# Attention and feed-forward in one kernel: the low part of q on GpSimd, and a later place for one pair's split

## The chip, the cores and the metric

The kernel runs on one core of a Trainium2 chip. The metric is the device time of one execution in microseconds. Five engines work side by side, each through its own queue in order: TensorE (PE in the profile; PEld is its weight load), VectorE (DVE), ScalarE (ACT), GpSimd (POOL) and SyncE (SP), which issues the DMAs. [...]

## The reference, cut to what matters

Causal attention over 4 batches, 12 heads, 448 positions and a head size of 64, and then, per position, a layer norm, two matrix products with a ReLU between them, and a residual:

```python
scores = scale * np.matmul(q, k.transpose(0, 1, 3, 2))
scores = np.where(mask, -1000000000.0, scores)
scores = scores - np.max(scores, axis=-1, keepdims=True)
attn = np.exp(scores)
attn = attn / (np.sum(attn, axis=-1, keepdims=True) + 1e-09)
x = np.matmul(attn, v)              # heads joined: 4 x 448 x 768
xn = (x - mu) / np.sqrt(var + 1e-06) * g_ln
out = x + np.maximum(xn @ w_ch1, 0.0) @ w_ch2    # 768 -> 3072 -> 768
```

## The kernel before, in words

**Slots.** The feed-forward part (`ffn`, L409) is cut into 48 slots per batch; a slot is 18 matmuls with 448 columns, and needs one half tile of weights. The main loop (L489) goes through slot numbers: negative ones are the head, in which batch 0's attention runs alone, and slots 0 to 191 carry the feed-forward of batches 0 to 3. At each slot it records, in this order, the steps in `pre`, the weights' steps, 18 feed-forward matmuls, and the steps in `post`. Each engine then does its own instructions in the order in which they were recorded; so the slot of a step sets its place in every queue, and no more than that: when it runs is settled by semaphores. The attention of batch b+1 is laid over the feed-forward of batch b.

**Exact products from fp32r matmuls.** Matmul operands are split in a high part (a copy that rounds to fp32r) and a low part (the difference). Weights: `wh` on ACT (L122), `wl` on DVE (L126), one slot ahead of use; while batch 0's feed-forward runs, the weights are also converted from 64-bit words (ACT L99 and L103, DVE L110). The hidden layer: `hh` on ACT (L426), `hl` on DVE (L427), which reads PSUM. The layer norm's output: `xh` on ACT (L358), `xl` on GpSimd (L361).

**Queries and keys of batches 1 to 3.** One pair of heads is loaded as `qkraw` (128 partitions, 4 x 448: two heads of q, two of k, each held twice, in partitions 0 to 63 and 64 to 127). `split1` (L186) makes `qs` as a rounded copy on ACT and `kh` as a rounded cast on DVE. `split2` (L196) subtracts: the lower 64 partitions of `qs` become the low part of q (L200, DVE), and `kl` becomes the low part of k (L203, GpSimd). A scores matmul with `kh` and one with `kl` (L234) then give the product. `qs`, `kh`, `kl` and `qkraw` have one buffer each. There are 18 such pairs. Batch 0 does without a split.

**Softmax.** `scores` (L205) writes negated, masked scores and their minimum on DVE (L242); `exps` on ACT (L256); `norm` (L262) makes the reciprocal of the sum on DVE (L267, L268) and scales four rows of blocks, on GpSimd for batch 0 and on DVE for the others (L272). Then come transposes on PE (L288) whose results ACT or DVE copies out (`PT`, L291 or L293), and the product with v (`px`, L303).

**Where steps stand.** In `steps` (L366) a pair p of batches 1 to 3 has `load` at 6p-4, `split1` at 6p-2 and `split2` at 6p-1, counted in a time of its own. `add_batch` (L456) maps that to slots. For batch 1 the negative times, which are those of its first pair alone, are moved by `FIRST` = -20: its load stands at slot -24, `split1` at -22 and `split2` at -21, in the middle of batch 0's attention. Its scores begin at slot -9. Batch 0's fifth pair has its normalisations at slots -22 and -20, the sixth and last at -16 and -14.

Of the kernel before, what the change touches and what calls it, by code (L numbers as in the profile page):

```python
# [32 lines left out]
EARLY = 45  # L33
GAP = 6
FIRST = -20
SAT0, TAT0, NAT0, END0, EV0 = [-1, 0, 2, 2, 4], [7, 8, 9, 10, 11], [4, 6], 13, [1, 1, 0, 1, 0]
SAT, TAT, NAT, END, EV = [0, 0, 1, 1, 2], [3, 4, 4, 5, 5], [3, 4], 6, [1, 1, 0, 0, 0]
EV1 = [1, 1, 1, 1, 1]
# [9 lines left out]
def kernel(ctx, tc, qk, v, w1, w2, g, out):  # L48
    nc = tc.nc
# [27 lines left out]
    def load_raw(s):  # L77
        kind, i = order[s // 2]
        raw[s] = sb.tile([P, UH, 2], U32, tag="raw", name="raw", bufs=5)
        src = (w1 if kind == "w1" else w2)[i].bitcast(U32)  # L80
        nc.sync.dma_start(
            out=raw[s].rearrange("p a b -> p (a b)"), in_=src[:, s % 2 * UE:(s % 2 + 1) * UE]
        )
# [40 lines left out]
    def split2(s):  # L124
        wl[s] = sb.tile([P, UH], F32R, tag="wl", name="wl", bufs=4)
        nc.vector.tensor_tensor(  # L126
            out=wl[s], in0=w32[s], in1=wh[s].bitcast(F32), op=ALU.subtract
        )

    def weights_ahead(start):  # L130


        early = 4
        todo = {}

        def put(t, *fs):
            todo.setdefault(max(t, start), []).extend(fs)

        for s in range(B * ns):
            t = (-EARLY + GAP * s, *ELAG) if s < early else (s - 4, 1, 2, 3)  # L140
            put(t[0] + t[3], (split2, s))
            if s < ns:
                put(t[0], (convert1, s))
                put(t[0] + t[1], (convert2, s))
                put(t[0] + t[1] + 1, (keep, s))
                if s + 5 < ns:
                    put(t[0] + t[1] + 1, (load_raw, s + 5))
            elif s % 2 == 0:
                put(s - 8, (load_full, s))
            put(t[0] + t[2], (split1, s))  # L150
        rank = [split2, convert2, convert1, keep, load_raw, load_full, split1]
        for fs in todo.values():
            fs.sort(key=lambda f: rank.index(f[0]))
        return todo


    class Att:
# [38 lines left out]
        def split2(self, p):  # L196
            r = self.t.pop(("raw", p))
            qs, kh, kl = self.t["qk", p]
            rq, rk = r[:, 0:2, :], r[:, 2:4, :]
            nc.vector.tensor_tensor(  # L200
                out=qs[D:], in0=rq[D:], in1=qs[D:].bitcast(F32), op=ALU.subtract
            )
            nc.gpsimd.tensor_tensor(out=kl, in0=rk, in1=kh.bitcast(F32), op=ALU.subtract)  # L203
# [246 lines left out]
    with tc.manual_schedule():  # L450
        more_qk = sb.tile([P, KC, S], F32, tag="xh", name="more_qk", bufs=1)
        first_qk = sb.tile([P, HF, S], F32, tag="hh", name="first_qk")
        rest = sb.tile([P, HF * S], F32, tag="hl", name="rest")
        pre, post, att = {}, {}, {}

        def add_batch(b):  # L456
            att[b] = Att(b)
            first, second, end = att[b].steps()
            shift = b * ns - end - (1 if b else 0)

            def slot(t):
                if b != 1:
                    return t + shift
                if t < 0:
                    return t + FIRST
                return t - 2 + HOLE[0] if t <= 2 else t - 3 + HOLE[1]

            for mine, whole in ((first, pre), (second, post)):
                for t, fs in mine.items():
                    whole.setdefault(slot(t), []).extend(fs)  # L470
            return slot(min(min(first), min(second)))

        start = add_batch(0)
        for p in range(NP):
            att[0].load(p)
            if p >= 2:
                load_raw(p - 2)
        nc.sync.dma_start(out=g_sb, in_=g)
        make_identity(nc, ident)
        nc.gpsimd.memset(mask, 0.0)  # L480
        nc.gpsimd.affine_select(
            out=mask[:, S - C:], in_=mask[:, S - C:], compare_op=ALU.is_ge, fill=-8.0e9,
            base=0, pattern=[[-1, C]], channel_multiplier=1,
        )
        nc.gpsimd.memset(mhalf, -0.5)
        for s in range(4, 5):
            pre.setdefault(start + 6 + 4 * s, []).append((load_raw, (s,)))
        feed, ahead = None, weights_ahead(start)
        for s in range(start, B * ns):  # L489
            for b in range(1, B):  # L490
                if b not in att and s >= (b - 1) * ns - (-start if b == 1 else 8):
                    assert add_batch(b) >= s, (b, s)
            for f, args in pre.get(s, []):
                f(*args)
            for f, x in ahead.get(s, []):
                f(x)
            if s >= 0:
                if s == 0:
                    hh = sb.tile([P, HF, S], F32R, tag="hh", name="hh")
                    hl = sb.tile([P, HF, S], F32R, tag="hl", name="hl")  # L500
                if s % ns == 0:
                    feed = ffn(att[s // ns], s, hh, hl)
                next(feed)
            for f, args in post.get(s, []):
                f(*args)
        for _ in feed:
            pass
# [33 lines left out]
```

## Time and profile before

| | |
|---|---|
| median of 3 runs | 919.53 us (918.36 to 921.22) |
| the profiled execution | 919.61 us, span 917.8 us |
| PE busy | 897.9 us (98%), 4864 matmuls |
| PEld busy | 790.2 us (86%) |
| DVE busy | 553.8 us (60%) |
| ACT busy | 452.8 us (49%) |
| POOL busy | 121.8 us (13%) |

Busy shares are means over stages that differ. The head, up to some 80 us, is batch 0's attention; the stretch to some 300 us is batch 0's feed-forward with the conversion of the weights and batch 1's attention; then three more feed-forwards follow, two of them with attention beside them. PE's matmuls are pipelined and their ends are modelled, so its busy time hides small waits; those show in the idle time ahead of a weight load.

### The profile page before, as it was taken

What the parts mean: (1) busy time and instruction counts of PE and PEld (TensorE: products, weight loads), DVE (VectorE), ACT (ScalarE), POOL (GpSimd) and SP (SyncE); (2) the same over time, 40 slices, a digit from 0 to 9 for tenths busy, and PEclk for the clock granted to TensorE, in tenths of its full rate; (3) what the DMA queues carried; (4) which work ended last, traced back from release to release, by engine and by line L of the source; (5) the groups of instructions that cost most, each with busy time, mean ns of one, the idle gap of its engine ahead of it and who ended that gap; (6) DMA issues with size and microseconds to landing.
All of it is one profiled execution on the core that took longest, in us unless ns stands there. A gap on an engine that the chain in (4) does not pass through costs nothing.

```text
span 917.8 us, 12820 instructions
## 1 busy us (share of the span) xinstructions
PE 897.9 (98%) x4864; PEld 790.2 (86%) x4864; DVE 553.8 (60%) x1208; ACT 452.8 (49%) x907; POOL 121.8 (13%) x115
## 2 busy tenths in 40 slices
PE   6988999999999999999999999999999999999998
PEld 4656889888899988988889998888988999999997
DVE  4877788777778566655664676556664634333431
ACT  5955888778865544444442355433542333222320
POOL 5543111101021111100102210011100200000000
PEclk9998999999999999999999999999999999999999
DMA  9920778787778643333313634343222343323210
GB/s 245 338 76 22 287 260 281 282 305 248 254 258 272 232 154 110 109 123 119 103 48 123 214 126 151 120 152 111 84 96 77 120 148 116 120 104 104 103 65 31
DMA packets 35246, 144.36 MB, mean 157 GB/s; under 512 B 4080, under 2 KB 8688, under 8 KB 35184
## 3 DMA queue, kind: packets, MB, share of 16 engines
q1 hardware_dynamic: 35184, 143.54, 45.2%
q8 instruction: 38, 0.62, 0.3%
q14 instruction: 24, 0.20, 0.1%
HBM read 119.15 MB, written 24.38 MB: 156 GB/s over the span
## 4 chain that ended last, share of the span: by engine, by line
PE 88%; ACT 5%; DVE 4%; DMA 1%; issue 1%; SPq 1%; POOL 0%; ACTq 0%
PE po L440 38%; PE ph L421 34%; PE px L303 5%; PE sc L234 4%; PE pt L288 4%; ACT P L256 2%; PE pln L316 1%; DMA raw<-w_dram 1%; PE sc L227 1%; ACT w L99 1%; ACT bits L103 1%; ACT wh L122 1%; DVE P L272 1%; DVE hl L427 1%; DVE wl L126 1%
## 5 line engine op out<-in xcount | busy, mean ns | idle before, releaser
L421 PE MATMUL ph<-xh,wh 128*128 128x448 f32 x576 | 214.5, 372 | 1.4 <-ACT xh L358 1.4
L440 PE MATMUL po<-hh,wh 128*128 128x448 f32 x576 | 214.1, 372 | 0.0
L421 PE MATMUL ph<-xl,wh 128*128 128x448 f32 x576 | 211.7, 368 | 0.5 <-POOL xl L361 0.5
L421 PE MATMUL ph<-xh,wl 128*128 128x448 f32 x576 | 211.3, 367 | 0.2
L440 PE MATMUL po<-hh,wl 128*128 128x448 f32 x576 | 210.7, 366 | 0.0
L440 PE MATMUL po<-hl,wh 128*128 128x448 f32 x576 | 210.6, 366 | 0.0
L427 DVE SCALAR_TENSOR_TENSOR hl<-ph,hh 128x448 fp32r<-128x448 f32 x96 | 59.8, 624 | 145.6 <-ACT hh L426 145.6
L122 ACT ACTIVATE wh<-full 128x768 fp32r<-128x768 f32 x144 | 119.3, 838 | 53.7 <-PE po L440 50.8
L126 DVE TENSOR_TENSOR wl<-full,wh 128x768 fp32r<-128x768 f32 x144 | 136.4, 953 | 0.8 <-ACT wh L122 0.5
L426 ACT ACTIVATE hh<-ph 128x448 fp32r<-128x448 f32 x96 | 52.0, 543 | 153.4 <-PE ph L421 153.2
L256 ACT ACTIVATE P<-P,nm 112x448 f32<-112x448 f32 (+3 forms) x176 | 91.7, 523 | 68.0 <-DVE nm L242 68.0
L421 PEld LDWEIGHTS ph<-xh,wl 128*128 128x128 f32 x576 | 108.6, 189 | 10.6 <-DVE wl L126 2.2
L421 PEld LDWEIGHTS ph<-xh,wh 128*128 128x128 f32 x576 | 108.7, 189 | 10.3 <-ACT xh L358 1.7
L421 PEld LDWEIGHTS ph<-xl,wh 128*128 128x128 f32 x576 | 108.7, 189 | 8.9 <-POOL xl L361 1.0
L440 PEld LDWEIGHTS po<-hh,wl 128*128 128x128 f32 x576 | 108.1, 188 | 9.2 <-DVE wl L126 0.4
L440 PEld LDWEIGHTS po<-hh,wh 128*128 128x128 f32 x576 | 108.2, 188 | 8.5
L440 PEld LDWEIGHTS po<-hl,wh 128*128 128x128 f32 x576 | 108.4, 188 | 8.2
L242 DVE CUSTOM_DVE_ANT_0 P<-sc,mask 112x448 f32<-112x448 f32 (+3 forms) x176 | 70.6, 444 | 51.9 <-PE sc L234 39.6
L203 POOL TENSOR_TENSOR kl<-qkraw,kh 128x896 fp32r<-128x896 f32 x18 | 51.8, 2878 | 377.0 <-DVE kh L193 370.3
L444 DVE TENSOR_TENSOR xT<-po,xT 128x448 f32<-128x448 f32 x48 | 29.9, 623 | 112.7 <-PE po L440 112.7
L288 PE MATMUL pt<-ident,P 112*112 112x112 f32 x440 | 55.1, 262 | 3.8 <-ACT PT L291 2.6
L288 PEld LDWEIGHTS pt<-ident,P 112*112 112x112 f32 x440 | 46.9, 134 | 13.5 <-ACT PT L291 4.1
(63 smaller groups left out, 941.8 us busy)
## 6 DMA issues: line engine op xcount, KB each, us to landing
full<-scratch SPq DMA_DIRECT2D x72, 768.0 KB, 4.2
raw<-w_dram SPq DMA_DIRECT2D x48, 768.0 KB, 5.7
scratch<-w SPq DMA_DIRECT2D x48, 384.0 KB, 2.9
qkraw<-qk_dram SPq DMA_DIRECT2D x18, 896.0 KB, 7.5
out_dram<-xT SPq DMA_DIRECT2D x24, 224.0 KB, 2.0
vt<-v_dram SPq DMA_DIRECT2D x18, 224.0 KB, 5.4
first_qk<-qk_dram SPq DMA_DIRECT2D x8, 224.0 KB, 5.5
rest<-v_dram SPq DMA_DIRECT2D x6, 224.0 KB, 7.8
```

Source lines behind the costliest of these rows:

```text
L122: nc.scalar.activation(out=wh[s], in_=w32[s], func=ACTF.Copy)
L126: nc.vector.tensor_tensor(out=wl[s], in0=w32[s], in1=wh[s].bitcast(F32), op=ALU.subtract)
L203: nc.gpsimd.tensor_tensor(out=kl, in0=rk, in1=kh.bitcast(F32), op=ALU.subtract)
L234: nc.tensor.matmul(pt[:, o:o + n], lhsT=qs[:, h, C * i:C * i + C], rhs=kk[:, h, :n], start=(part == 0), stop=(part == 1),)
L242: nc.vector.tensor_tensor_reduce(out=self.t["P", p, h][:, OFF[i]:OFF[i + 1]], in0=pt[:, o:o + n], in1=mask[:, S - n:], op0=ALU.add, op1=AL ...
L256: nc.scalar.activation(out=pp, in_=pp, func=ACTF.Exp, scale=-1.0, bias=nm[:, x:x + 1], accum_out=self.t["sm", p, h][:, i:i + 1],)
L288: nc.tensor.transpose(pt[:, o:o + C], pp[:, a:a + C], ident[:C, :C])
L303: nc.tensor.matmul(px[D * h:D * h + D, C * j:], lhsT=vt[:, h, j, :], rhs=self.t.pop(("PT", p, h, j)), start=(j == 0), stop=(j == NC - 1),)
L421: nc.tensor.matmul(pm[y], lhsT=w[:, c * P:c * P + P], rhs=z[:, c, :], start=(c == 0 and i == 0), stop=(c == KC - 1 and i == 2),)
L426: nc.scalar.activation(out=hh[:, x + y, :], in_=pm[y], func=ACTF.Relu)
L427: nc.vector.scalar_tensor_tensor(out=hl[:, x + y, :], in0=pm[y], scalar=0.0, in1=hh[:, x + y, :].bitcast(F32), op0=ALU.max, op1=ALU.subtract,)
L440: nc.tensor.matmul(pm, lhsT=w[:, o:o + P], rhs=z[:, x, :], start=(x == 0 and i == 0), stop=(x == HF - 1 and i == 2),)
```

## The change

`split2` issues both subtractions on GpSimd, that for q first, in all 18 pairs. For the first pair of batch 1 a table `PARTS` replaces the shift: `split1` stands at slot -18 instead of -22, and `split2` at -13 instead of -21. Its load stays at -24.

```diff
 FIRST = -20
+PARTS = [-18, -13]
...
             qs, kh, kl = self.t["qk", p]
             rq, rk = r[:, 0:2, :], r[:, 2:4, :]
-            nc.vector.tensor_tensor(
+            nc.gpsimd.tensor_tensor(
                 out=qs[D:], in0=rq[D:], in1=qs[D:].bitcast(F32), op=ALU.subtract
             )
             nc.gpsimd.tensor_tensor(out=kl, in0=rk, in1=kh.bitcast(F32), op=ALU.subtract)
...
                 if t < 0:
-                    return t + FIRST
+                    return PARTS[t + 2] if t >= -2 else t + FIRST
```

With the added line, the line numbers of the changed kernel are one higher. The names in the following pieces: `rest` and `P` hold the softmax rows, `sc` is a scores tile in PSUM, `nm` the minimum that L242 reads out after each piece of scores.

DVE in the head, after the reciprocals of the fifth pair's first head; before:

```order
L193 CAST kh<-qkraw 128x896
L242 ISA rest,nm<-sc,mask 112x112
L242 ISA nm 112x1
L242 ISA rest,nm<-sc,mask 112x336
L242 ISA nm 112x1
L200 TENSOR_TENSOR qs<-qkraw,qs 64x896
L293 COPY PT<-pt 112x448
L242 ISA P,nm<-sc,mask 112x448
```

and with the change:

```order
L243 ISA rest,nm<-sc,mask 112x112
L243 ISA nm 112x1
L243 ISA rest,nm<-sc,mask 112x336
L243 ISA nm 112x1
L294 COPY PT<-pt 112x448
L243 ISA P,nm<-sc,mask 112x448
```

The cast to `kh` and the subtraction are gone from in front of the `PT` copy; the cast stands further on, behind the scores of the next groups, and the subtraction is not on DVE any more. PE's queue and SP's queue have the same order as before, and on ACT the copy to `qs` moves back by nine instructions.

GpSimd in the head; before, from the first pair's `kl` on:

```order
L203 TENSOR_TENSOR kl<-qkraw,kh 128x896
L272 TENSOR_SCALAR rest<-rest,r 112x112
L272 TENSOR_SCALAR rest<-rest,r 112x224
L272 TENSOR_SCALAR rest<-rest,r 112x448
L272 TENSOR_SCALAR rest<-rest,r 112x336
L272 TENSOR_SCALAR P<-P,r 112x112
L272 TENSOR_SCALAR P<-P,r 112x224
L272 TENSOR_SCALAR P<-P,r 112x448
L272 TENSOR_SCALAR P<-P,r 112x336
```

and with the change, from the last head's normalisation on:

```order
L273 TENSOR_SCALAR P<-P,r 112x112
L273 TENSOR_SCALAR P<-P,r 112x224
L273 TENSOR_SCALAR P<-P,r 112x448
L273 TENSOR_SCALAR P<-P,r 112x336
L201 TENSOR_TENSOR qs<-qkraw,qs 64x896
L204 TENSOR_TENSOR kl<-qkraw,kh 128x896
L329 TENSOR_TENSOR ve<-ve,mhalf 112x4
L362 TENSOR_TENSOR xl<-xg,xh 128x448 x6
```

Both subtractions of the first pair stand behind the last normalisation of batch 0 and in front of the layer norm's `ve`.

DVE at the third pair of batch 1, from the cast on; before:

```order
L193 CAST kh<-qkraw 128x896
L126 TENSOR_TENSOR wl<-w_1177,wh 128x768
L110 SCALAR_TENSOR_TENSOR w_1282<-w_1282,bits 128x768
L427 SCALAR_TENSOR_TENSOR hl<-ph,hh 128x448
L200 TENSOR_TENSOR qs<-qkraw,qs 64x896
L126 TENSOR_TENSOR wl<-w_1231,wh 128x768
```

and with the change:

```order
L194 CAST kh<-qkraw 128x896
L127 TENSOR_TENSOR wl<-w_1177,wh 128x768
L111 SCALAR_TENSOR_TENSOR w_1282<-w_1282,bits 128x768
L428 SCALAR_TENSOR_TENSOR hl<-ph,hh 128x448
L127 TENSOR_TENSOR wl<-w_1231,wh 128x768
L111 SCALAR_TENSOR_TENSOR w_1333<-w_1333,bits 128x768
```

The `wl` that stood behind the subtraction follows `hl` directly. At the fourth and fifth pair there is no `hl` in this place: the cast is followed by a `wl`, a conversion, the subtraction (before only), a second `wl` and a second conversion. GpSimd has `qs` and then `kl` at each of these pairs.

## Rows read from the trace of the kernel before

**Rows 1.** the page: the span
```profile
span 917.8 us, 12820 instructions
```

**Rows 2.** who waited for whom, PE only: us in total, times, longest us
```profile
PE px L303 <- DVE PT L293: 2.4, 1, 2.4
```

**Rows 3.** the chain that ended last, 30 to 100 us: start us, us, what
```profile
46.22 0.85 ACT qs L192
47.09 0.15 DVE qs L200
47.24 3.90 issue
51.14 0.64 DVE PT L293
```

**Rows 4.** timeline of POOL, 40 to 96 us: start, us, engine, line, operation
```profile
45.98 2.14 POOL L272 TENSOR_SCALAR rest<-rest,r 112x112 f32<-112x112 f32 x4 [2.09 <-DVE r L268]
48.08 2.08 POOL L203 TENSOR_TENSOR kl<-qkraw,kh 128x896 fp32r<-128x896 f32 x1
58.96 3.82 POOL L272 TENSOR_SCALAR P<-P,r 112x112 f32<-112x112 f32 x8 [3.61 <-DVE r L268]
```

**Rows 5.** one stretch: us, busy us of PE, PEld, DVE, ACT, POOL, then PEclk
```profile
53.00:57.00 4.00, 4.00 (x16) 2.98 (x15) 1.90 (x9) 3.12 (x12) 2.35 (x4) 0.57 0.61 242
```

**Rows 6.** timelines of DVE (54 to 58 us) and PE (67 to 69)
```profile
56.05 0.39 DVE L242 CUSTOM_DVE_ANT_0 P<-sc,mask 112x224 f32<-112x224 f32 x1 [1.86 <-PE sc L227]
...
67.91 0.36 PE L234 MATMUL sc<-kl,qs 128*112 128x448 f32 x1
```

**Rows 7.** POOL instructions by shape: xcount, busy us, mean ns, idle before
```profile
L203 POOL TENSOR_TENSOR kl<-qkraw,kh 128x896 fp32r<-128x896 f32 x18 | 51.8, 2878 | 377.0 <-DVE kh L193 370.3 <-PE ph L421 6.8
L171 POOL MEMSET first_qk<- 64x448 f32 x4 | 1.9, 466 | 0.4 <-POOLq L530 0.3
L480 POOL MEMSET mask<- 112x448 f32 x1 | 0.5, 476 | 0.0
```

**Rows 8.** timeline of DVE, 120 to 130 us
```profile
125.27 0.62 DVE L427 SCALAR_TENSOR_TENSOR hl<-ph,hh 128x448 fp32r<-128x448 f32 x1
125.91 2.40 DVE L200 TENSOR_TENSOR qs<-qkraw,qs 64x896 fp32r<-64x896 f32 x1
128.32 0.96 DVE L126 TENSOR_TENSOR wl<-w,wh 128x768 fp32r<-128x768 f32 x1
```

**Rows 9.** timeline of POOL, 90 to 330 us
```profile
94.24 2.63 POOL L203 TENSOR_TENSOR kl<-qkraw,kh 128x896 fp32r<-128x896 f32 x1 [6.77 <-PE ph L421]
...
123.76 3.60 POOL L203 TENSOR_TENSOR kl<-qkraw,kh 128x896 fp32r<-128x896 f32 x1 [26.88 <-DVE kh L193]
...
151.32 3.59 POOL L203 TENSOR_TENSOR kl<-qkraw,kh 128x896 fp32r<-128x896 f32 x1 [23.96 <-DVE kh L193]
...
210.75 3.60 POOL L203 TENSOR_TENSOR kl<-qkraw,kh 128x896 fp32r<-128x896 f32 x1 [25.89 <-DVE kh L193]
...
300.30 2.79 POOL L203 TENSOR_TENSOR kl<-qkraw,kh 128x896 fp32r<-128x896 f32 x1 [11.68 <-DVE kh L193]
...
326.05 2.72 POOL L203 TENSOR_TENSOR kl<-qkraw,kh 128x896 fp32r<-128x896 f32 x1 [22.96 <-DVE kh L193]
```

**Rows 10.** timeline of PE's weight loads, at six pairs
```profile
99.32 0.19 PEld L421 LDWEIGHTS ph<-xh,wl 128*128 128x128 f32 x1
...
129.33 0.19 PEld L421 LDWEIGHTS ph<-xh,wl 128*128 128x128 f32 x1 [0.46 <-DVE wl L126]
...
157.55 0.19 PEld L440 LDWEIGHTS po<-hh,wl 128*128 128x128 f32 x1
...
216.32 0.19 PEld L421 LDWEIGHTS ph<-xh,wl 128*128 128x128 f32 x1 [0.45 <-DVE wl L126]
...
305.80 0.19 PEld L421 LDWEIGHTS ph<-xh,wl 128*128 128x128 f32 x1
...
331.95 0.19 PEld L421 LDWEIGHTS ph<-xh,wl 128*128 128x128 f32 x1
```

## Prediction

> **What bounds the kernel.** The profiled execution took 919.61 us, with a span of 917.8 us [rows 1]; the median of the three runs is 919.53 us, so the sum below is made against 919.61 and nothing has to be added for the difference. About 0.3% (2.8 us) is what a measurement of this kernel can tell from no change. I read the waits of PE first: beside the first load there is one wait of any size in the whole execution, 2.4 us before the `px` matmuls, ended by a `PT` copy on DVE [rows 2]. PE otherwise works nearly without a break (DVE's weight halves come late to a few weight loads, below), so a change on DVE, ACT or POOL is worth something where it removes that wait, and costs something where it makes a new one.
>
> The chain of waits names what stands in front of the 2.4 us [rows 3]: ACT's copy `qs` (0.85 us), then DVE's subtraction for the low part of `qs`, in which 3.90 us go by as "issue", then the `PT` copy that PE needs. That subtraction is 64x896 elements and lasts 0.95 us where nothing is in its way (below); here it lasts from 47.09 to 51.11. GpSimd's timeline says why [rows 4]: four normalisations run from 45.98 to 48.12, and `kl` follows without a gap, 48.08 to 50.16. DVE's operation ends 0.95 us after `kl`. So an operation with two SBUF inputs on DVE stands still while GpSimd works in SBUF, and it did not get in between two GpSimd operations that followed each other closely. [...]
>
> **The change, part by part.**
>
> *The first pair's parts, 18 slots ahead instead of 22, and 13 instead of 21.* ACT's `qs` copy, DVE's `kh` cast and the two subtractions leave the stretch at 46 to 51 us. DVE's `PT` copy then stands behind scores that are ready, and PE's 2.4 us go. With them goes the reason for the low clock: 4.0 us at 0.57 [rows 5] are 4.0 x 0.43 = 1.7 us of lost matmul time. Together 2.4 + 1.7 = **4.1 us**. Floor: the 2.4 us alone, if the clock falls for another reason. Ceiling: the 0.85, 0.15 and 3.90 us of the chain, 4.9 us. I take 4.1, since both parts of it have their rows. What comes back later is covered: ACT's 0.85 us leaves its queue before one `PT` copy and comes back before another, nine operations on, so that ACT's own chain is as long as it was at the end of the head; DVE's `kh` cast now stands in front of the scores of the last pair, where DVE waited 1.86 us for PE [rows 6]. GpSimd's `qs` and `kl` come after its last normalisations, which end at 58.96 + 3.82 = 62.78 [rows 4]; two subtractions of 2.08 us bring that to 66.94, and the first matmul that reads `kl` starts at 67.91 [rows 6]. Both move forward together, so 1.0 us is spare; if the cover were gone, each microsecond would be PE's. On SP nothing moves.
>
> *The other 17 pairs: one subtraction from DVE to GpSimd.* What it costs GpSimd: the 128x896 `kl` has a mean of 2.88 us, but that holds waits; with none it takes 2.08 us (at 48.08) [rows 4, 7]. The new one has the same 896 elements in 64 partitions. GpSimd's own rows say whether half the partitions halve the time: a memset of 64x448 takes 466 ns, one of 112x448 476 ns [rows 7]. So I take 2.08 us, the bound below being 1.04. GpSimd has the time; but it holds up DVE while it works, and this is where the cost lies.
>
> Take the pair at 123 us. `kl` is asked for at 123.76, and DVE goes on through two more two-input operations without GpSimd getting in; at 125.27 DVE begins `hl`, which reads PSUM, and 2.08 us later, at 127.36, `kl` ends. DVE's `qs` begins at 125.91, stands still until 127.36 and ends 0.95 us later; the next `wl` ends at 129.28 [rows 8, 9]. PE loads it at 129.33, 0.46 us late [rows 10]. After the change DVE has `wl` in place of `qs`, at 125.9, and GpSimd has `qs` and `kl` in its queue. ACT's copy is done while DVE is still in its normalisations, so `qs` is asked for in the middle of DVE's row and waits, as `kl` did, until `hl` at 125.27. Then GpSimd works 4.16 us without a gap, and `wl` waits for all of it. So PE gets `wl` at the end of `kl` before, plus 2.08 (the second subtraction), plus 0.96 (`wl`), plus 0.05 to the load. By pair, from [rows 9, 10]:
> - 94.24: 96.87 + 3.09 = 99.96 against 99.32, costs 0.64 us.
> - 123.76: 130.45 against 129.33, costs 1.12 us.
> - 210.75: 217.44 against 216.32, costs 1.12 us.
> - 300.30: 306.18 against 305.80, costs 0.38 us.
> - 326.05: 331.86 against 331.95, still in time by 0.09 us; this and the ten pairs after it are counted as nothing, and this is the tightest cover in the sum.
>
> The pair at 151.32 and the one like it at 181 us are let off: behind DVE's weight conversion stands not `hl` but the next `wl` and conversion, so DVE, going from one two-input operation to the next as at 123.76, makes the `wl` that PE wants next before GpSimd gets in, and what is then held up is the `wl` of the slot after. Were they not let off, the first would cost 154.91 + 3.09 - 157.55 = 0.45 us [rows 9, 10], the other about as much. Loss 0.64 + 1.12 + 1.12 + 0.38 = **3.3 us**, at most 4.3. Who else waits: the first scores of a pair need both low parts, which are two slots of PE work ahead of them; the load of the next pair's `qkraw` waits 2 us longer, three slots ahead of its use. Neither is near.
>
> Sum: 919.61 - 4.1 + 3.3 = **918.8 us**.
>
> [...] At 47.09 DVE waited through the end of a normalisation (48.12) and through `kl` behind it [rows 3, 4]: the turn stayed with GpSimd over the boundary of two instructions. [...] The row decides for the forecast.
>
> **Rivals.**
> 1. *DVE gets a turn between GpSimd's `qs` and `kl`.* Then the first of the two stands where `kl` alone stood, `wl` follows at its end without DVE's own `qs` ahead of it, and PE's load comes at 127.36 + 0.96 + 0.05 = 128.37 instead of 129.33: the loss is gone and the waits of 0.46 and 0.45 us [rows 10] with it. 919.61 - 4.1 - 0.9 = 914.6 us. For it: a DVE operation that arrives just then could win; against it: DVE's 4.02 us at 47.09.
> 2. *GpSimd's `qs` gets its turn inside DVE's row of normalisations*, since it is now asked for as soon as ACT is done and not after `kh`. It decides from the point where `kh` and the `wl` behind it start 2.08 us late. At the pairs of 123 and 210 us, where PE waits for `wl` already, that is 2.08 us in place of 1.12 each, 1.9 more; at the two let off up to 2.08 each, of which I take half, 2.1 more. 918.8 + 4.0 = 922.8 us, slower than before. Against it: at 123.76 GpSimd waited through two DVE operations [rows 8, 9].
> 3. *Sixty-four partitions take half the time.* With 1.04 us the costs above shrink to 0.08 us at two pairs: 919.61 - 4.1 + 0.2 = 915.7 us. Against it: the two memsets.
>
> That the change does not do what it says is excluded by the order: all 18 subtractions stand on GpSimd, and the first pair's behind the last normalisation.
>
> **How the numbers follow.** Forecast 0.55, with its own range 917.2 (gain at its ceiling) to 920.4 (a loss of 4.3 and a gain of 3.5); rival 1 0.25, rival 2 0.12, rival 3 0.08. Faster by over 0.3% is under 916.9: rivals 1 and 3, and 0.03 of the forecast's edge, 0.36. Slower by over 0.3% is over 922.4: a little over half of rival 2 and 0.03 for a stretch that I have not seen, 0.10. The rest, 0.54, lies within. The range takes in rivals 1 and 3 and stops short of rival 2: 914.0 to 921.0.
>
> **What would show it.** Right: no PE wait over 1 us before `px` at 49 us and a clock of 1.00 from 53 to 57; the head, up to the first `ph` matmul, some 4 us shorter; GpSimd's `qs` at 2.1 us of work and `kl` right behind it; a `wl` at the 123 and 210 us pairs of some 3.5 to 4.5 us instead of 0.96, with a late weight load behind it; the weight conversion stretch, up to 300 us, 3 us longer. Wrong: a `wl` that stands between `qs` and `kl` (rival 1), a `kh` or normalisation of 2.4 us or more on DVE (rival 2), a `qs` of 1 us on GpSimd (rival 3), or PE waiting for `kl` before the first scores.

## The result, and the profile after

The changed kernel took 927.86 us (median of 4 runs, 927.69 to 930.9) against 920.38 us for the kernel before in the same comparison: a ratio of 1.0094, with a 95% interval from 1.0073 to 1.0114 (the two medians alone give 0.8%). The forecast was 918.8 us and the range ended at 921.0; slower by over 0.3% had been given 0.10. The profiled execution took 927.78 us with a span of 926.0 us, 8.2 us more than before [rows 1].

The page of the profile after: the span, the busy line (busy us, share of the span, instructions) and GpSimd's share in 40 slices of the span, in tenths.

```profile
span 926.0 us, 12865 instructions
PE 898.7 (97%) x4864; PEld 787.1 (85%) x4864; DVE 561.7 (61%) x1190; ACT 453.0 (49%) x907; POOL 163.9 (18%) x133
POOL 5555023302022122210202320121200300000000
```

PE has the same work to do; GpSimd has 42 us more, in the stretches with attention. Waits of PE behind DVE have appeared (who waited for whom, PE only: us in total, times, longest):

```profile
PE ph L422 <- DVE wl L127: 4.5, 8, 0.6
PE pt L289 <- DVE P L273: 3.1, 5, 1.1
PE po L441 <- DVE wl L127: 1.7, 3, 0.6
```

The 2.4 us in front of `px` [rows 2] are gone; in their place PE waits eleven times for `wl` and five times for the normalised rows `P`.

**The head.** Clock and busy time of the stretch that was at 0.57 before [rows 5], now:

```profile
53.00:57.00 4.00, 4.00 (x30) 2.83 (x29) 1.96 (x10) 2.74 (x10) 2.87 (x7) 1.00 0.00 0
```

The `px` product with the old wait inside it, and its neighbours, on PE's timeline, before:

```profile
39.68 2.11 PE L303 MATMUL px<-PT,rest 112*64 112x448 f32 x16
...
47.87 1.53 PE L303 MATMUL px<-PT,rest 112*64 112x448 f32 x6
51.82 1.35 PE L303 MATMUL px<-PT,rest 112*64 112x336 f32 x10 [2.42 <-DVE PT L293]
...
59.12 2.37 PE L303 MATMUL px<-PT,rest 112*64 112x448 f32 x16
```

and after:

```profile
39.18 2.11 PE L304 MATMUL px<-PT,rest 112*64 112x448 f32 x16
...
47.36 2.11 PE L304 MATMUL px<-PT,rest 112*64 112x448 f32 x16
...
54.24 2.43 PE L304 MATMUL px<-PT,rest 112*64 112x448 f32 x16
```

From the start of the second to the start of the third it was 11.25 us (the second stands in two parts, with the wait between them) and is 6.88 us: 4.4 us won where 4.1 were forecast. The other gain lies around it. Some 0.5 us lie behind, where PE's granted clock over 70 to 92 us is 0.92 instead of 0.84. And 0.5 us are there already at the first of the three products (39.18 against 39.68), ahead of the first instruction that the change moves, so they are not its work: in the profiled executions of the kernels in this document that product starts anywhere from 37.55 to 39.68 us, with the same work in front of it. Why it varies is open; a difference of up to 2 us between two profiles in the head can be this.

**The rest.** To see where the time goes, take the weight load that is the first of a slot to read `wl`. The slots with loads at 305.80 and 331.95 stand in [rows 10]; the first and a late one before:

```profile
81.45 0.34 PEld L421 LDWEIGHTS ph<-xh,wl 128*128 128x128 f32 x1
...
665.13 0.19 PEld L421 LDWEIGHTS ph<-xh,wl 128*128 128x128 f32 x1
```

and the same four slots after:

```profile
75.97 0.19 PEld L422 LDWEIGHTS ph<-xh,wl 128*128 128x128 f32 x1
...
305.43 0.19 PEld L422 LDWEIGHTS ph<-xh,wl 128*128 128x128 f32 x1
...
332.74 0.19 PEld L422 LDWEIGHTS ph<-xh,wl 128*128 128x128 f32 x1
...
673.30 0.19 PEld L422 LDWEIGHTS ph<-xh,wl 128*128 128x128 f32 x1
```

So the changed kernel is 5.5 us ahead at slot 0, 0.4 us ahead when batch 1's pairs and the first of batch 2 are through (305.43 against 305.80), 0.8 us behind one pair later, and 8.2 us behind at the last pair of batch 3 (673.30 against 665.13), after which nothing changes. The pairs up to 305 us cost 5.1 us, where 3.3 were forecast; the eleven behind them cost 8.5 us, where nothing was.

One of these pairs on GpSimd after, the one at 326.05 before [rows 9]:

```profile
324.26 2.12 POOL L201 TENSOR_TENSOR qs<-qkraw,qs 64x896 fp32r<-64x896 f32 x1 [19.95 <-ACT qs L193]
327.62 2.71 POOL L204 TENSOR_TENSOR kl<-qkraw,kh 128x896 fp32r<-128x896 f32 x1 [1.24 <-DVE kh L194]
```

and DVE beside it (four normalisation operations, `kh`, two `wl`):

```profile
323.84 3.10 DVE L273 TENSOR_SCALAR P<-P,r 112x112 f32<-112x112 f32 x4
326.86 0.61 DVE L194 CAST kh<-qkraw 128x896 fp32r<-128x896 f32 x1
327.40 0.94 DVE L127 TENSOR_TENSOR wl<-full,wh 128x768 fp32r<-128x768 f32 x1
329.33 1.81 DVE L127 TENSOR_TENSOR wl<-full,wh 128x768 fp32r<-128x768 f32 x1
```

Before, DVE's timeline of the same pair:

```profile
324.19 1.20 DVE L272 TENSOR_SCALAR P<-P,r 112x112 f32<-112x112 f32 x4
325.30 0.62 DVE L193 CAST kh<-qkraw 128x896 fp32r<-128x896 f32 x1
325.83 0.96 DVE L126 TENSOR_TENSOR wl<-full,wh 128x768 fp32r<-128x768 f32 x1
329.73 0.96 DVE L126 TENSOR_TENSOR wl<-full,wh 128x768 fp32r<-128x768 f32 x1
```

The row of normalisations lasts 3.10 us instead of 1.2, and it is GpSimd's `qs` that has got in: asked for at 324.26, it is done at 326.38, and DVE's third operation (one of the four in the first row), which begins at 324.28, lasts until 326.63. `kh` ends at 327.47, 1.9 us later than behind a row of 1.2 us, and the `wl` behind it (328.34) comes too late for PE, which waits 0.57 us for it. Grouped by shape, DVE's 448-column normalisation before:

```profile
L272 DVE TENSOR_SCALAR P<-P,r 112x448 f32<-112x448 f32 x36 | 16.1, 448 | 0.0
```

and after:

```profile
L273 DVE TENSOR_SCALAR P<-P,r 112x448 f32<-112x448 f32 x36 | 37.0, 1028 | 0.0
```

Thirty-six of them, and a mean that has gone from 448 to 1028 ns: 36 times 0.58 us is 20.9 us, and it lies on eleven of them, which stood still some 1.9 us each. At a twelfth pair the 224-column operation did (2.20 us at 176.71, where it needs 0.33). GpSimd's two operations by shape, after:

```profile
L201 POOL TENSOR_TENSOR qs<-qkraw,qs 64x896 fp32r<-64x896 f32 x18 | 44.4, 2469 | 336.9 <-ACT qs L193 336.4 <-POOL xl L362 0.4
L204 POOL TENSOR_TENSOR kl<-qkraw,kh 128x896 fp32r<-128x896 f32 x18 | 49.3, 2739 | 15.8 <-DVE kh L194 15.4
```

### The profile page after: what moved, and what is told of

The parts are those of the page before. It is cut to its first block, busy times and chain, and to the rows that moved or that the text cites. A ratio compares the mean times of both kernels' runs of the same rounds, so it can differ in the third digit from the quotient of the medians.

```text
span 926.0 us, 12865 instructions
## 1 busy us (share of the span) xinstructions
PE 898.7 (97%) x4864; PEld 787.1 (85%) x4864; DVE 561.7 (61%) x1190; ACT 453.0 (49%) x907; POOL 163.9 (18%) x133
## 4 chain that ended last, share of the span: by engine, by line
PE 80%; DVE 9%; ACT 8%; issue 1%; DMA 1%; SPq 1%; POOL 0%; ACTq 0%; DVEq 0%
PE po L441 36%; PE ph L422 30%; PE px L304 4%; PE sc L235 4%; DVE P L273 4%; PE pt L289 3%; ACT P L257 2%; DVE wl L127 1%; ACT w L100 1%; ACT bits L104 1%; PE pln L317 1%; DVE hl L428 1%; DMA raw<-w_dram 1%; ACT rest L257 1%; ACT PT L292 1%
## 5 line engine op out<-in xcount | busy, mean ns | idle before, releaser
L127 DVE TENSOR_TENSOR wl<-full,wh 128x768 fp32r<-128x768 f32 x144 | 148.6, 1038 | 0.5 <-ACT wh L123 0.5
L201 POOL TENSOR_TENSOR qs<-qkraw,qs 64x896 fp32r<-64x896 f32 x18 | 44.4, 2469 | 336.9 <-ACT qs L193 336.4
L273 DVE TENSOR_SCALAR P<-P,r 112x112 f32<-112x112 f32 (+3 forms) x144 | 66.5, 524 | 1.3
```

Source lines behind the costliest of these rows:

```text
L127: nc.vector.tensor_tensor(out=wl[s], in0=w32[s], in1=wh[s].bitcast(F32), op=ALU.subtract)
L201: nc.gpsimd.tensor_tensor(out=qs[D:], in0=rq[D:], in1=qs[D:].bitcast(F32), op=ALU.subtract)
L273: eng.tensor_scalar(out=pp, in0=pp, scalar1=r[:, i:i + 1], scalar2=1.0, op0=ALU.mult, op1=ALU.mult,)
```

## The experiments

Two theories. **A, the turn:** `qs` on GpSimd is asked for as soon as ACT's copy is done, which is in the middle of DVE's normalisations; it gets in there, and `kh` and `wl` come late. **B, occupancy:** a pair costs more because GpSimd works in SBUF for twice as long, whenever it starts.

**1. The places alone** (q back on DVE for all pairs).

```diff
-            nc.gpsimd.tensor_tensor(
+            nc.vector.tensor_tensor(
                 out=qs[D:], in0=rq[D:], in1=qs[D:].bitcast(F32), op=ALU.subtract
             )
```

> The table of places alone: q's low part is back on DVE for all 18 pairs. Theory A (the turn): GpSimd's q operation is asked for as soon as ACT's copy is done, often just ahead of one of DVE's normalisation operations, which then stands still about 1.9 us with kh and wl behind it; twelve pairs lose 0.8 to 1.5 us each so, 13.2 us in all, against 5.5 us won in the head. Theory B (occupancy): the pairs lose because GpSimd works in SBUF for twice as long per pair, whenever it starts. Both expect no loss at the pairs here. In the head, DVE's q operation now meets kl behind the last normalisations and stands still up to 2 us: between 914.9 us (head gain of 5.5 whole) and 918 us (3 of it given back).

914.91 us against 919.44, ratio 0.9953 (0.9935 to 0.9970). The places alone make the kernel faster, by about the gain that the forecast had for them. Their table is not what made the changed kernel slow.

**2. The engine alone** (the first pair's split at its old slots).

```diff
-                    return PARTS[t + 2] if t >= -2 else t + FIRST
+                    return t + FIRST
```

> q's low part on GpSimd for all pairs, the first pair's split left at slots -22 and -21. Both theories: the pairs lose 13 us as in the changed kernel. Head: DVE no longer stands still 4 us, but GpSimd's two operations stand between the fifth pair's two normalisations, so that the second of these comes some 2 us later; I expect 1 to 3 us of the head's 5.5 us. 930 to 933 us.

932.01 us, ratio 1.0136 (1.0118 to 1.0154). The engine costs 12.6 us by itself. In its profile the pairs lose 15.3 us from slot 0 on, not the 13 that were expected: at the pair of 210 us PE's clock falls as well (0.79 over 212 to 220 us), which costs some 1.7 us. Of the 2.8 us that this profile is ahead at slot 0, 2.0 are the early start (the first `px` product above stands at 37.68 here). The differences of experiments 1 and 2, -4.5 and +12.6 us, add up to the 7.5 us of the change within 0.6 us.

**3. k's subtraction ahead of q's.** Same work, same engines, same places; two statements of `split2` change their order.

```diff
+            nc.gpsimd.tensor_tensor(out=kl, in0=rk, in1=kh.bitcast(F32), op=ALU.subtract)
             nc.gpsimd.tensor_tensor(
                 out=qs[D:], in0=rq[D:], in1=qs[D:].bitcast(F32), op=ALU.subtract
             )
-            nc.gpsimd.tensor_tensor(out=kl, in0=rk, in1=kh.bitcast(F32), op=ALU.subtract)
```

> The changed kernel with k's subtraction ahead of q's in GpSimd's queue, so that q's cannot be asked for before kh is cast; the work on every engine is the same. Theory A: DVE's normalisations do not stand still any more; what is left is wl waiting for both operations, the 3.3 us that the prediction worked out for batch 1, so 917 to 919 us. Theory B: no change against the changed kernel, 927 to 928 us.

912.85 us, ratio 0.9930 (0.9915 to 0.9945): 15 us less than the changed kernel, and below all that either theory had. B falls: GpSimd does as much as in the changed kernel. The pair of above, on GpSimd and on DVE:

```profile
319.57 2.62 POOL L201 TENSOR_TENSOR kl<-qkraw,kh 128x896 fp32r<-128x896 f32 x1 [21.54 <-DVE kh L194]
322.26 2.70 POOL L202 TENSOR_TENSOR qs<-qkraw,qs 64x896 fp32r<-64x896 f32 x1
```

```profile
317.60 1.19 DVE L273 TENSOR_SCALAR P<-P,r 112x112 f32<-112x112 f32 x4
321.78 1.21 DVE L127 TENSOR_TENSOR wl<-full,wh 128x768 fp32r<-128x768 f32 x1
```

The row of normalisations lasts 1.19 us again, since `qs` stands behind `kl`, and `kl` waits for `kh`. And `wl`, which I had waiting for both operations, begins at 321.78, waits for `kl` alone and ends at 322.99, while `qs` waits for it: it begins at 322.26 and lasts 2.70 instead of 2.1 us. DVE got in between two operations of GpSimd that are 0.08 us apart. That is the mechanism of the prediction's first rival, in another kernel.

**4. q on GpSimd for the first pair alone.**

```diff
+            eng = nc.gpsimd if self.b == 1 and p == 0 else nc.vector
-            nc.gpsimd.tensor_tensor(
+            eng.tensor_tensor(
                 out=qs[D:], in0=rq[D:], in1=qs[D:].bitcast(F32), op=ALU.subtract
             )
```

> The table of places, with q's low part on GpSimd for the first pair alone and on DVE for the other 17. Both theories: the head's 5.5 us whole and no loss at the pairs, 914 to 916 us. If it stays above 918, part of the head's gain came from elsewhere.

914.14 us, ratio 0.9942 (0.9927 to 0.9957). With the places set, it matters little in the head which engine does the first pair's q (914.14 against 914.91); and the kernel with k first is ahead by another 1.3 us, of which 0.9 stand at the pairs of 123 and 210 us, where PE's weight load comes 0.4 us earlier each.

**5. Both subtractions on DVE** (the engine of both statements is `nc.vector`).

> The table of places, and both subtractions of all 18 pairs on DVE; GpSimd touches no q or k. DVE gives up its standstill (0.3 to 2 us a pair) and gets kl (0.95 us) instead. Theory A: wl comes earlier where kl blocked it (pairs of batch 1) and about as before elsewhere, 913 to 916 us. If DVE's own time is what matters, wl comes 0.9 us later at the pairs of batches 2 and 3 whose spare time is 1.25 us, still no loss.

916.35 us against 919.17, ratio 0.9979 (0.9958 to 1.0000), hardly to be told from no change. A miss by 0.4 us: at the pairs nothing is lost, as expected, but in the head, by the weight loads of slot 0, only 4.5 us are won, where experiment 4 has 5.8.

**6 and 7. Ask later.** The changed kernel, with one and with three tiny copies on ACT ahead of the copy to `qs` in 17 pairs; `tiny` is a tile of 4 columns that nobody reads.

```diff
+            if self.b > 1 or p:
+                for _ in range(3):
+                    nc.scalar.copy(out=tiny, in_=ident[:, 0:4])
             nc.scalar.activation(out=qs, in_=rq, func=ACTF.Copy)
```

> The changed kernel with one tiny ACT copy ahead of the copy to qs in 17 pairs, so that GpSimd's q operation is asked for some 0.1 to 0.2 us later and nothing else moves. Theory A, sharpened: who waits while the other works does not get in between two operations that follow each other closely, and who asks just at the boundary wins; the request then falls into the middle of a normalisation operation, waits until DVE leaves its row, and DVE's normalisations do not stand still. q's operation lasts 4 to 6 us instead of 2.1, and the late pairs lose little: 915 to 920 us. Theory B, or a turn that goes by who waits longest: 927 to 929 us, as the changed kernel.

> The same with three tiny copies, a request 0.3 to 0.5 us later than in the changed kernel. Theory A: if it falls on the next boundary (some 0.35 us later) the next normalisation operation stands still and the 13 us are back; if it falls inside an operation, the time is that of one tiny copy. Theory B: 927 to 929 us.

One copy: 930.14 us, ratio 1.0135 (1.0097 to 1.0172), above the ranges of both theories. Three: 916.74 us, ratio 0.9981 (0.9963 to 1.0000). More work on ACT, and 13 us less. The copies moved the request within the row of normalisations, and its place there decided. With one copy, the same pair on GpSimd and DVE:

```profile
324.93 2.34 POOL L204 TENSOR_TENSOR qs<-qkraw,qs 64x896 fp32r<-64x896 f32 x1 [19.10 <-ACT qs L196]
```

```profile
324.41 3.05 DVE L276 TENSOR_SCALAR P<-P,r 112x112 f32<-112x112 f32 x4
327.39 0.62 DVE L197 CAST kh<-qkraw 128x896 fp32r<-128x896 f32 x1
```

The request, moved by 0.1 us, falls 0.08 us into the third operation. I expected it to wait until DVE's row is through; it waited 0.2 us and got in ahead of the fourth. So in this detail A was wrong: the waiting GpSimd did get in, at the next boundary, which was one in front of a normalisation. With three copies:

```profile
319.32 3.60 POOL L205 TENSOR_TENSOR qs<-qkraw,qs 64x896 fp32r<-64x896 f32 x1 [20.43 <-ACT qs L197]
323.00 2.71 POOL L208 TENSOR_TENSOR kl<-qkraw,kh 128x896 fp32r<-128x896 f32 x1
```

```profile
318.34 1.19 DVE L277 TENSOR_SCALAR P<-P,r 112x112 f32<-112x112 f32 x4
319.45 0.62 DVE L198 CAST kh<-qkraw 128x896 fp32r<-128x896 f32 x1
322.51 1.22 DVE L128 TENSOR_TENSOR wl<-full,wh 128x768 fp32r<-128x768 f32 x1
```

Now the request (319.32) falls into the fourth and last normalisation. It does not get in ahead of `kh` or `wl`, which follow it; it waits until that `wl` is done (320.94) and DVE has a pause, and `qs` is done at 322.92. The normalisations last 1.19 us, and this pair costs PE nothing. The expectation had the time for a request inside an operation, but not that it was the last one of the row: of the 17 pairs one, with its request at 173.69 in the third operation, still loses (its row lasts 3.06 us). Both kernels also lose 1.7 to 1.9 us behind 690 us, where no pair is left; that was not followed up.

**8. k first, without the places.** Experiment 3's order with the return of experiment 2.

> k's subtraction ahead of q's on GpSimd, the first pair's split left at slots -22 and -21. The 17 later pairs as in the kernel with k first (0 to 1 us won). Head: DVE's standstill of 4 us is gone, but the second normalisation of the fifth pair waits for both GpSimd operations, as with the engine alone, where 2.8 us of the head were won. 916 to 918 us.

918.08 us against 919.17, ratio 1.0000 (0.9979 to 1.0021): no change to be told from none. The engine, in the right order, costs nothing. The profile is 2.5 us ahead at slot 0, but 2.1 of that are the early start (the first `px` product stands at 37.55), and 1.3 are lost again by slot 1, with a clock of 0.77 over 70 to 92 us against 0.84 before. In the stretch itself little is won: DVE's 4 us are gone, but PE now waits 0.7 us for a `PT` copy on ACT and 1.4 us for the normalisation that stands behind both subtractions on GpSimd. So most of the expectation's 2.8 us for the head was not the engine's. The gain of experiment 3 is that of the places.

**9. Normalisations without a scalar operand.**

```diff
+                if self.b:
+                    n = OFF[i + 1] - OFF[i]
+                    eng.tensor_tensor(out=pp, in0=pp, in1=r[:, i:i + 1].to_broadcast([C, n]), op=ALU.mult)
+                    continue
                 eng.tensor_scalar(
```

> What the two kernels with a later request left open: GpSimd got in at the boundary in front of a normalisation operation, 0.1 to 0.3 us after it had asked, and not in front of a cast or a weight operation, where it waited 3.6 us and more. Here the changed kernel's normalisations of batches 1 to 3 multiply by a broadcast tensor instead of a per-partition scalar operand; each operation on DVE is 0.05 to 0.2 us longer. If the scalar operand opens the boundary, q's operation now waits until DVE has done kh and wl (3 to 6 us long), no normalisation stands still, and the time is 916 to 920 us. If normalisations can be broken into for another reason, one still stands still 1.9 us at twelve pairs: 927 to 931 us.

935.16 us, ratio 1.0179 (1.0146 to 1.0211), above both ranges. The scalar operand is not it: the 448-column operation alone, which needs 0.62 us where it is left alone, has this mean by shape:

```profile
L275 DVE TENSOR_TENSOR P<-P,r 112x448 f32<-112x448 f32 x36 | 43.5, 1208 | 0.0
```

Why `qs` got in ahead of normalisations, and not ahead of the casts and weight operations of its pairs, stays open. The kernel before has more rows on it. At the pair of 151.32, where `kl` lasts until 154.91 [rows 9], on DVE:

```profile
151.10 0.95 DVE L126 TENSOR_TENSOR wl<-w,wh 128x768 fp32r<-128x768 f32 x1
151.97 0.95 DVE L110 SCALAR_TENSOR_TENSOR w<-w,bits 128x768 uint32<-128x768 uint32 x1
152.95 2.90 DVE L200 TENSOR_TENSOR qs<-qkraw,qs 64x896 fp32r<-64x896 f32 x1
```

`kl` did not get in ahead of the conversion and did get in ahead of DVE's subtraction of 64 partitions, which stood still until 154.91. And GpSimd's `xl` did get in ahead of a conversion, on GpSimd and on DVE:

```profile
266.34 1.22 POOL L361 TENSOR_TENSOR xl<-xg,xh 128x448 fp32r<-128x448 f32 x1 [3.19 <-ACT xh L358]
```

```profile
265.56 0.95 DVE L126 TENSOR_TENSOR wl<-w,wh 128x768 fp32r<-128x768 f32 x1
266.43 1.94 DVE L110 SCALAR_TENSOR_TENSOR w<-w,bits 128x768 uint32<-128x768 uint32 x1
```

The same stands there five times more up to 288 us, and once ahead of `kh` (1.61 us at 515.88, beside an `xl` at 515.78). The normalisations have 112 partitions, the casts and weight operations 128, so partitions alone do not decide it.

## Why the prediction was wrong

**Right: what bounds the head.** The 2.4 us wait and the low clock went together: in experiments 2 and 8, where PE waits 2.1 us there in two pieces, the clock over 53 to 57 us is 0.69 and 0.61, and it is 1.00 in the changed kernel and in experiments 1, 3 and 4, where the wait is gone. What lowers it is not shown. Of the changed kernel's 5.5 us up to slot 0, 4.4 are this stretch, for 4.1 forecast; experiment 1 had the same with q left on DVE. (The lower end of the forecast's own range does not come out of its terms: 919.61 - 4.9 + 3.3 is 918.0 and not 917.2. Nothing here turns on it.) The first pair's q and k were ready before the first scores, as forecast.

**Right: the price of the operation.** `qs` with 64 partitions is at least as long as `kl`: 2.08 us at the first pair, where nothing is in its way, and 2.1 us at most others. Rival 3 is out.

**Wrong: "`qs` is asked for in the middle of DVE's row and waits, as `kl` did, until `hl`".** This is the step that failed. The request was where the forecast had it, 0.13 us after ACT's copy, in the row of normalisations. It did not wait. The row that I took this from, `kl` at 123.76 [rows 9], shows GpSimd waiting through a `wl` and a conversion on DVE:

```profile
123.00 0.62 DVE L193 CAST kh<-qkraw 128x896 fp32r<-128x896 f32 x1
123.54 0.95 DVE L126 TENSOR_TENSOR wl<-w,wh 128x768 fp32r<-128x768 f32 x1
124.40 0.95 DVE L110 SCALAR_TENSOR_TENSOR w<-w,bits 128x768 uint32<-128x768 uint32 x1
```

None of the rows showed a GpSimd operation that is asked for during normalisations on DVE, for in the kernel before `kl` waits for `kh`, which stands behind them. I carried a row over to operations that it did not show. What the runs showed in its place: at twelve of the 17 pairs `qs` got in ahead of a normalisation, which then lasted some 1.9 us longer (324.28 to 326.63 above), with `kh` and `wl` as late behind it. The forecast's way did occur, once: at the pair that stood at 151.32, the request fell into the last of the four operations (GpSimd, then DVE's normalisations, `kh`, the last of four weight operations, and the `xT` addition from PSUM):

```profile
147.43 6.33 POOL L201 TENSOR_TENSOR qs<-qkraw,qs 64x896 fp32r<-64x896 f32 x1 [22.62 <-ACT qs L193]
153.84 2.12 POOL L204 TENSOR_TENSOR kl<-qkraw,kh 128x896 fp32r<-128x896 f32 x1
```

```profile
146.57 1.20 DVE L273 TENSOR_SCALAR P<-P,r 112x112 f32<-112x112 f32 x4
147.68 0.63 DVE L194 CAST kh<-qkraw 128x896 fp32r<-128x896 f32 x1
150.82 0.96 DVE L111 SCALAR_TENSOR_TENSOR w<-w,bits 128x768 uint32<-128x768 uint32 x1
153.87 0.62 DVE L445 TENSOR_TENSOR xT<-po,xT 128x448 f32<-128x448 f32 x1 [2.09 <-PE po L441]
```

`qs` waited until 151.7, when DVE had nothing to do for 2.1 us, its 6.33 us being that wait and 2.1 us of work, and this pair cost nothing, as it had been let off. Of the 17 pairs that are left, the five whose request came with no normalisation left to begin (this one, and those that stood at 300, 381, 517 and 599 us) cost nothing, and the other twelve 0.9 to 1.5 us each.

**Right in kind, wrong in place: rival 2.** It named this mechanism, "`qs` gets its turn inside DVE's row of normalisations", and was priced at 922.8 us, since I applied it to the four pairs of batch 1 with late weights and left the pairs from 326.05 on at nothing. Their spare time was worked out for a `wl` that is late once, by GpSimd's operations; with `kh` 1.9 us late as well, the `wl` right behind `kh` is what PE waits for (about 1.1 us per pair by the weight loads). Eight of those pairs made 8.5 of the 13.6 us. Priced for all twelve at the 1.04 us that I took for a pair let off, the rival would have stood at 919.61 - 4.1 + 12.5, about 928; that this is so near to 927.86 is partly luck, since the 1.04 had no row. Its sign, a normalisation of 2.4 us or more, came at 2.36 us.

**The end of an instruction.** I let one row decide what happens there, DVE waiting through a normalisation and `kl` on GpSimd [rows 4]: 4.02 us for a subtraction whose shortest of 18 lasts 1.09 us. In experiments 3 and 6 the waiting engine did get in at the end of an instruction (`qs` 0.2 us after it had asked in experiment 6, DVE's `wl` after waiting 0.26 us in experiment 3). The row of before, the 6.33 us above and experiment 7 show boundaries at which it did not. So in these runs the end of an instruction was a chance for the one that waits and not a promise; the range should have taken in both at every pair. The profile names no releaser for these waits: of DVE's 4.02 us it gives 3.90 as "issue" [rows 3], and the normalisation's 2.36 us as busy time. So the sentence at the start, that semaphores settle when a step runs, leaves out what this case turned on.

## What to carry to other kernels

An operation moved to an engine that has time still has a moment at which it asks, here 0.13 us after its input was there: where the two engines hold each other up, as GpSimd and DVE did here (a normalisation of 2.36 us instead of 0.45), look at what the engine that it leaves does at that moment, and if need be put the operation behind another whose input comes only after that work. Here the order of two statements on an engine that is idle four fifths of the time was worth 15 us (experiment 3), and the kernel with k first (912.85 us) is the fastest of all that ran. And a tight cover found for one late step (0.09 us at the pairs from 326 on) is to be priced for the rivals too, times the number of its repetitions.

## What the runs showed of the hardware

GpSimd's `qs` got in ahead of DVE's normalisation operations in the changed kernel and in experiments 6 and 9 (in experiment 7 at one pair), whether these had a scalar operand or a broadcast tensor, after a wait of at most 0.13 us in the changed kernel and of 0.2 us at the pair shown of experiment 6. `qs` and `kl` did not get in between a normalisation and the cast behind it, nor between cast, weight subtraction and weight conversion, in the rows shown of the kernel before, of the changed kernel and of experiment 7 (waits of 1.5 to 4.2 us); `xl` did, at six conversions and one cast of the kernel before (1.22 us long, where the shortest of 24 took 1.17). DVE got in between two GpSimd operations 0.08 us apart (experiment 3), and not between two without a gap (4.02 us where the shortest of 18 took 1.09, in the kernel before). And a delay of some 0.45 us in one engine's request, from one tiny copy on ACT to three, changed the whole kernel's time by 13 us.
